# Compute engines in program order from the first network matmul on, with the steps of the transform laid out anew

## The chip, the core and the metric

The kernel runs on one core of one Trainium2 chip. The metric is the device time of one execution in microseconds, the median of several runs. Engines are TensorE (PE in the rows, its weight loads PEld), VectorE (DVE), ScalarE (ACT), GpSimd (POOL) and SyncE (SP, which here only issues DMAs).

## The reference

Three stages follow one another on 8 x 3072 tokens of 256 channels:

```
X = rfft(x, axis=1);  y = irfft(X * (filt_r + i filt_i))      # a long convolution, per batch row
h = y @ w_in                                                  # 256 -> 2048
g = h if h >= 1;  0 if h <= -1;  else (h + 1)^2 / 4
x2 = g @ w_out                                                # 2048 -> 256
e = argmax(x2 @ w_gate);  p = softmax(x2 @ w_gate)[e]          # one of 8 experts per token
out = p * (relu(x2 @ w1[e]) @ w2[e])                           # 256 -> 1024 -> 256
```

Everything is float32 at both ends.

## The kernel before

**Stages.** The transform runs one batch row at a time, as eight "transform units" u = 0 to 7. Unit 0 comes alone, ahead of the network. Then the network (the two dense layers and the routing) runs over 48 blocks of 512 tokens, and beside the blocks of unit u-1's tokens the matmuls of unit u are slipped in. After the last block come the experts, tile by tile of 256 tokens.

**Precision.** Each float32 operand is split in a high and a low part (f16 in the network and the experts, a rounded float32 in the transform), and three matmuls (high x high, high x low, low x high) stand for one. The splitting is ACT, DVE and POOL work.

**The network's loop.** A "unit" n is 256 tokens by 512 hidden columns; there are 384, of four *steps* each, 1536 steps in all. Step 4n and 4n+1 are the two halves of the first layer (`l1`, L520, 12 matmuls each, into a two-bank PSUM tile `hps`); `act1` (L535) clips on DVE (L538) and squares on ACT (L539); `act2` (L542) takes the maximum on DVE (L544), makes `gh` on ACT (L547) and `gl` on POOL (L548). Steps 4n+2 and 4n+3 are the second layer (`l2`, L551) of unit n-2, 12 matmuls each, into the two PSUM banks `yps`. After the last unit of half a block `finish` (L570) copies `yps` to `ysb`, one bank by ACT (L574), one by DVE (L575), and at the end of a block it sets events for scaling, routing (`route1`, `route2`) and scatters of the rows.

**Events.** `ev(h, f)` puts f into step h; `fire(h)` (L931) calls what lies there, between the halves of the layers. Every piece of the transform, the routing and the experts' weight preparation is such an event. In a transform unit the A pieces (`a_load`, `a_run`, six groups) transform along one axis; the B pieces (16 groups) load a table, the filter and A's result, split it (`b_split`, L397), transform it (`b_fwd`, L401), copy it turned to `xs` (ACT, L412, L413), multiply with the filter (`b_mul`: DVE L420, POOL L421), add (`b_add`: DVE L427), split the sum into `yh` and `yl` (L324 on ACT, L325 on DVE), and transform back (`b_inv`, L430). `a_inv` (L502) makes the network's input of a block. All of these, the scales and `route2` share two PSUM banks (`fps`, L165).

**What sets the order.** The program order is that of the events, but the planner that lays out each engine's queue from simulated times may move instructions past each other; only some are pinned by `keep_in_program_order`. The events' offsets are the constants at L28 to L34: B's inverse comes 5 steps after its forward transform (LG), A's load 3 steps ahead of its use (LA), `z_load` 14 and `a_inv` 11 and 6 steps ahead of the block (ZO), `route2` 4 steps after the block and one after `route1`'s second part (FO).

Of the kernel before, what the change touches and what calls it, by code (L numbers as in the profile page):

```python
# [31 lines left out]
UA = (9, 4.7)  # L32
CVA = 4
LA, LB, LC, SA, HB, SB_, LG = 3, 14, 9, 7.4, 59.8, 7.4, 5  # L34
# [95 lines left out]
def tile_kernel(ctx, tc, x, w_in, w_out, w_gate, w1, w2, cst, tab, fil, out):  # L130
# [37 lines left out]
    if True:  # L168
# [71 lines left out]
        def bmax(m, n):  # L240
            k = m.shape[0]
            p = fps()
            PE.transpose(p[0:n, 0:k], m, c[0:k, C_ID:C_ID + k])
            q = fp.tile([n, 1], F32, tag="bm", name="bm")
            V.tensor_reduce(q, p[0:n, 0:k], axis=AX.X, op=ALU.max)
            if n > 1:
                d = fp.tile([n, n], F32, tag="bd", name="bd")
                V.tensor_scalar(d, c[0:n, C_ID:C_ID + n], q, None, op0=ALU.mult)
                q = d
            p = fps()  # L250
            PE.matmul(p[:, 0:n], lhsT=c[0:n, C_ONE:C_ONE + 128], rhs=q)
            return p[:, 0:n]
# [30 lines left out]
        def scales(u):  # L283
            zm = sq[u]
            m = fp.tile([96, 1], F32, tag="zr", name="zr")
            V.tensor_reduce(m, zm, axis=AX.X, op=ALU.max)
            q = fp.tile([128, 12], F32, tag="sq", name="sq")
            qi = q.bitcast(I32)
            pow2(q[:, 0:1], bmax(m, 1), -30, 100)
# [22 lines left out]

        def warp(h):
            k, r = divmod(h - W1, 32)
            return int(32 * k + W1 + r * (32 - WL) / 32)
# [5 lines left out]
        def split(X, t, th, tl):  # L321
            h = qp.tile(list(t.shape), F32R, tag=th, name=th, bufs=bufs.get(th))
            l = qp.tile(list(t.shape), F32R, tag=tl, name=tl, bufs=bufs.get(tl))
            A.activation(h, t, AF.Copy)  # L324
            X.tensor_tensor(l, t, h.bitcast(F32), op=ALU.subtract)  # L325
            return h, l
# [19 lines left out]
        def pin(u, g, *a):  # L346
            i = SP.dma_start(*a)
            if u == 1 and g < 3:
                tc.keep_in_program_order(i)

        def fft_unit(u, ha, sa, hb, sb, lag):
# [4 lines left out]
            def a_load(g):  # L356
                xi = alt(u, g, [128, 4, D], "xi", (qp, "xi"), (fp, "zt"), (fp, "xl"), (qp, "xg"), (fp, "zt"), (fp, "xl"))
                pin(u, g, xi, x[u].rearrange("(p s) d -> p s d", s=S2)[:, 4 * g:4 * g + 4, :])
                st["x", g] = xi

            def a_run(g):
                xi = st.pop(("x", g))
                if u:
                    xg, xr = split(G, xi, "xg", "xr")
                ao = alt(u, g, [128, 4, D], "ao", (qp, "ao"), (fp, "xh"), (qp, "xr"), (fp, "xh"))
                for i in range(2):
                    p = ups(u)
                    s = slice(2 * i, 2 * i + 2)
                    if u:
                        mm(p, cah, cal, xg[:, s].rearrange("p b d -> p (b d)"), xr[:, s].rearrange("p b d -> p (b d)"))  # L370
                    else:
                        mm(p, c[:, C_A:C_A + 128], None, xi[:, s].rearrange("p b d -> p (b d)"), None)
                    A.activation(ao[:, s].rearrange("p b d -> p (b d)"), p, AF.Copy)
                SP.dma_start(s1v[:, 4 * g:4 * g + 4], ao)

            def b_load(g):
                if u:
                    tt = qp.tile([128, 2, 2, 224], F32R, tag="tt", name="tt")
                    G.dma_start(tt, tab[g, :, 1:3])
# [3 lines left out]
                tf = alt(u, g, [128, 2, 2 * D], "tf", (qp, "tf"), (fp, "xh"), (fp, "xl"))  # L383
                pin(u, g, *((tf, fil[g]) if u or g == 0 else (tf[0:64], fil[g, 0:64])))
                st["b", g] = (tt, tf)

# [10 lines left out]
            def b_split(g):  # L397
                tt, tf, t = st["b", g]
                st["b", g] += split(V, t, "ag", "al") if u else (None, None)

            def b_fwd(g):  # L401
                tt, _, t, ag, al = st["b", g]
# [13 lines left out]
            def b_mul(g):  # L416
                tf = st["b", g][1]
                pv, xs = st.pop(("p", g))
                xq = alt(u, g, [128, 2, D], "xq", (qp, "xq"), (fp, "gl"))
                V.tensor_tensor(xq, pv, tf[:, :, 0:D], op=ALU.mult)  # L420
                G.tensor_tensor(xs, xs, tf[:, :, D:], op=ALU.mult)  # L421
                st["q", g] = (xq, xs)

            def b_add(g):
                if u:
                    xq, xs = st["q", g]
                    V.tensor_tensor(xq, xq, xs, op=ALU.add)  # L427
                    st["q", g] = split(V, xq, "yh", "yl")

            def b_inv(g):  # L430
# [10 lines left out]
                z = alt(u, g, [96, 2, D], "z", (qp, "ao"), (qp, "xi"), (qp, "xg"), (qp, "xr"))  # L441
# [3 lines left out]
                V.tensor_reduce(sq[u][:, g:g + 1], z.rearrange("p q d -> p (q d)"), axis=AX.X, op=ALU.max, apply_absolute_value=True)  # L445
                SP.dma_start(s2v[8 * g:8 * g + 8].rearrange("(q p) s d -> (p s) q d", q=2), z)

            if u == 0:
# [16 lines left out]
                for g in range(NG):  # L465
# [4 lines left out]
                    at(t, (b_split, g), (b_fwd, g), (b_mul, g), (b_add, g))  # L470
# [4 lines left out]
                return  # L475
            for g in range(NA):
                h = warp(ha + sa * g)
                ev(h - LA, lambda g=g: a_load(g))
                ev(h, lambda g=g: a_run(g))
            for g in range(NG):  # L480
                h = warp(hb + g * sb)
                ev(h - LB, lambda g=g: b_load(g))
                ev(h - LB, lambda g=g: b_load2(g))
                ev(h - LC, lambda g=g: b_dup(g))
                ev(h - LC, lambda g=g: b_split(g))
                ev(h, lambda g=g: b_fwd(g))
                ev(h, lambda g=g: b_mul(g))
                ev(h, lambda g=g: b_add(g))
                ev(warp(hb + g * sb + lag), lambda g=g: b_inv(g))
# [4 lines left out]
        def z_load(k):  # L494
# [3 lines left out]
            if k < 2:  # L498
# [3 lines left out]
        def a_inv(k, kt):  # L502
# [8 lines left out]
            V.scalar_tensor_tensor(xl[:, kt, :], p, sx, xh[:, kt, :], op0=ALU.mult, op1=ALU.subtract)  # L511
# [58 lines left out]
        def finish(k, half, h):  # L570
# [7 lines left out]
            o = FO if k < NBLK - 1 else (0, 0, 0, 0, 2, 2, 2, 6, 5)  # L578
# [4 lines left out]
            ev(h + o[4], lambda: route2(k, 0))  # L583
            ev(h + o[5], lambda: route2(k, 1))
            ev(h + o[6], lambda: route1(k, 2))
            for j in range(4):
                ev(h + o[7] + o[8] * j, lambda j=j: hilo(k, j, 0))
                ev(h + o[7] + o[8] * j, lambda j=j: hilo(k, j, 1))
                ev(h + o[7] + 1 + o[8] * j, lambda j=j: scatter(k, j))
# [18 lines left out]
        def route1(k, i):  # L608
# [5 lines left out]
            if i == 0:  # L614
# [6 lines left out]
                tc.keep_in_program_order(V.memset(row[:, :, D + 2:ROW], 0.0))  # L621
# [70 lines left out]
        def wload(i):  # L692
            src, _, _, wi = wchunk(i % 64)
            t = fp.tile([128, 512], F32, tag="wst", name="wst", bufs=3)
            tc.keep_in_program_order(SP.dma_start(t if wi == 0 else t.rearrange("p (k d) -> p k d", d=D), src))
# [7 lines left out]
        def wscale():  # L703
            m = fp.tile([128, 2], F32, tag="wm", name="wm")
            V.tensor_reduce(m, wmax.rearrange("p (a b) -> p a b", a=2), axis=AX.X, op=ALU.max)
            p = fps()
# [9 lines left out]
            for a in range(2):  # L716
                V.tensor_scalar(dg[:, a, :], c[0:2, C_ID:C_ID + 2], m2[:, 2 + a:3 + a], None, op0=ALU.mult)
            p2 = fps()
# [19 lines left out]
        fft_unit(0, 0, 0, 0, 0, 0)  # L738
        z_load(0)
        scales(0)  # L740
        for f in range(UF):
            wi_split(f)
        for kt in range(2):
            a_inv(0, kt)
# [280 lines left out]
```

## Time and profile before

| | us |
|---|---|
| median of 3 runs | 3742.18 (3742.1 to 3750.3) |
| the profiled execution, its own time | 3752.54 |
| its span, first to last instruction | 3750.8 |
| PE busy | 3532.5 (94%) |
| DVE, ACT, POOL busy | 2459.9, 1807.8, 1671.1 |
| network stage (first network matmul to the last) | 140.0 to 2724.1 |

Busy is time in which at least one instruction of the engine was at work. "Idle before" in a row is the time that the engine stood still just ahead of the instructions of that row, and the arrow names what it waited for. PEclk is the share of full TensorE clock (2.4 GHz) that was granted.

### The profile page before, as it was taken

Reading aid. Unit: us, or ns where it says so; the run is one execution under the profiler, and the core shown is the slowest. Engines: PE = TensorE matmul, PEld = TensorE weight load, DVE = VectorE, ACT = ScalarE, POOL = GpSimd, SP = SyncE. Lnnn points to the kernel's source line nnn. Section 1 sums busy time; section 2 is a strip of 40 time slices with the busy share of each in tenths; the row PEclk is TensorE's granted clock in tenths of the full one; section 3 lists DMA queues with packets and bytes.
Section 4 is the critical chain, followed back from the end, with each engine's and each line's share of the span. In section 5 each row is a group of like instructions: output and inputs, shape, how many; then the busy total and the mean of one; then the engine's idle time right before and its main releaser. Section 6 shows DMA issues by size and latency. Waiting matters only on the chain. (4 is left out here: it accounts for less than half of the span.)

```text
span 3750.8 us, 75150 instructions
## 1 busy us (share of the span) xinstructions
PE 3532.5 (94%) x30690; PEld 3075.9 (82%) x30690; DVE 2459.9 (66%) x3830; ACT 1807.8 (48%) x2406; POOL 1671.1 (45%) x1154
## 2 busy tenths in 40 slices
PE   6799899999999999999999999999999999999998
PEld 4687787878778777888888788888888888888887
DVE  6678868887896887788688778867642333333222
ACT  4655555656555565665566566544422222222221
POOL 1355455555555555555555545544422222222222
PEclk7899999999999999999999999999999999999999
DMA  9345434433443443454344335301132222222221
GB/s 274 122 131 150 137 122 132 140 119 122 145 133 114 132 131 117 130 151 126 120 131 137 116 105 152 96 24 70 45 76 52 51 52 52 52 52 52 52 50 52
DMA packets 323821, 395.33 MB, mean 105 GB/s; under 512 B 163791, under 2 KB 250063, under 8 KB 322960
## 3 DMA queue, kind: packets, MB, share of 16 engines
q1 hardware_dynamic: 274848, 279.90, 26.1%
q0 software_dynamic: 48624, 110.58, 9.8%
q8 instruction: 243, 3.98, 0.5%
q14 instruction: 106, 0.87, 0.1%
HBM read 439.70 MB, written 120.49 MB: 149 GB/s over the span
## 5 line engine op out<-in xcount | busy, mean ns | idle before, releaser
L548 POOL TENSOR_TENSOR gl<-cl,gh 128x1024 f16<-128x1024 f32 x384 | 834.1, 2173 | 691.0 <-ACT gh L547 332.8
L531 PE MATMUL hps<-xh,wih 128*128 128x256 f16 x3072 | 841.6, 274 | 4.3 <-DVE cl L544 4.3
L531 PE MATMUL hps<-xl,wih 128*128 128x256 f16 x3072 | 841.2, 274 | 0.7 <-DVE xl L511 0.7
L531 PE MATMUL hps<-xh,wil 128*128 128x256 f16 x3072 | 841.0, 274 | 0.0
L561 PE MATMUL yps<-woh,gh 128*128 128x264 f16 x3072 | 730.1, 278 | 11.7 <-ACT ysb L574 6.6
L561 PE MATMUL yps<-wol,gh 128*128 128x264 f16 x3072 | 730.7, 279 | 0.0
L539 ACT ACTIVATE cl<-cl,sq 128x1024 f32<-128x1024 f32 x384 | 475.9, 1239 | 493.2 <-DVE cl L538 455.1
L561 PEld LDWEIGHTS <-gh 128*128 128x128 f16 x6144 | 592.5, 99 | 115.7 <-issue 21.9
L886 DVE SCALAR_TENSOR_TENSOR hl<-mh,hh 128x1024 f16<-128x1024 f32 x194 | 237.6, 1225 | 655.6 <-ACT hh L885 655.5
L531 PEld LDWEIGHTS <-wih 128*128 128x128 f16 x6144 | 595.9, 98 | 86.4 <-DVE cl L544 5.8
L544 DVE SCALAR_TENSOR_TENSOR cl<-hps,sq,cl 128x1024 f32<-128x1024 f32 x384 | 491.2, 1279 | 198.8 <-ACT cl L539 197.3
L538 DVE TENSOR_SCALAR cl<-hps,sq 128x1024 f32<-128x1024 f32 x384 | 513.2, 1337 | 118.6 <-PE hps L531 114.7
L547 ACT ACTIVATE gh<-cl 128x1024 f16<-128x1024 f32 x384 | 404.9, 1055 | 312.9 <-DVE cl L544 304.6
L877 PE MATMUL mh<-xt,wslot 128*128 128x256 f16 x4656 | 540.2, 273 | 0.0
L885 ACT ACTIVATE hh<-mh 128x1024 f16<-128x1024 f32 x194 | 198.4, 1023 | 655.0 <-PE mh L877 450.9
L877 PEld LDWEIGHTS <-wslot 128*128 128x128 f16 x4656 | 455.6, 98 | 52.9 <-issue 0.2
L561 PE MATMUL yps<-woh,gl 128*128 128x264 f16 x3072 | 420.8, 278 | 1.6 <-POOL gl L548 1.6
L900 PE MATMUL my<-wslot,hh 128*128 128x256 f16 x3104 | 371.4, 273 | 0.4 <-issue 0.3
L561 PEld LDWEIGHTS <-gl 128*128 128x128 f16 x3072 | 299.5, 98 | 52.5 <-POOL gl L548 2.9
L900 PEld LDWEIGHTS <-hh 128*128 128x128 f16 x3104 | 303.7, 98 | 36.0 <-issue 1.0
L531 PEld LDWEIGHTS <-wil 128*128 128x128 f16 x3072 | 301.8, 98 | 37.8 <-issue 0.9
L677 POOL DMA_INDIRECT rows<-row,posi x192 | 206.0, 1073 | 270.6 <-DMA rows<-row,posi 97.6
(202 smaller groups left out, 4361.1 us busy)
## 6 DMA issues: line engine op xcount, KB each, us to landing
tf<-in_fil_dram SPq DMA_DIRECT2D x113, 512.0 KB
tt<-in_tab_dram POOLq DMA_DIRECT2D x112, 448.0 KB
wst<-in_w_dram SPq DMA_DIRECT2D x128, 256.0 KB
xi<-in_x_dram SPq DMA_DIRECT2D x48, 512.0 KB
scr<-ao SPq DMA_DIRECT2D x48, 512.0 KB
a<-scr SPq DMA_DIRECT2D x128, 192.0 KB
scr<-z SPq DMA_DIRECT2D x128, 192.0 KB
zt<-scr SPq DMA_DIRECT2D x48, 512.0 KB
```

Of the source, the lines that this page charges most:

```text
L531: PE.matmul(p[:, i, :], lhsT=w[:, kt, f * 128:(f + 1) * 128], rhs=xx[:, kt, s], start=a == 0, stop=a == 5)
L538: V.tensor_scalar(cl, p, q[:, 5:6], q[:, 3:4], op0=ALU.max, op1=ALU.min)
L539: A.activation(cl, cl, AF.Square, bias=q[:, 11:12], scale=q[:, 4:5])
L544: V.scalar_tensor_tensor(cl, p, q[:, 7:8], cl, op0=ALU.mult, op1=ALU.max)
L547: A.activation(gh, cl, AF.Copy)
L548: G.tensor_tensor(gl, cl, gh, op=ALU.subtract)
L561: PE.matmul(yps[j][:, 0:WO], lhsT=gg[:, i, j * 128:(j + 1) * 128], rhs=w[:, f, :], start=f == 0 and first, stop=f == NF - 1 and gg is gl)
L677: G.indirect_dma_start(out=rows, out_offset=IOA(ap=posi[:, j:j + 1], axis=0), in_=row[:, j, :], in_offset=None, bounds_check=NROWS - 1, oo ...
L877: PE.matmul(p[:, i, :], lhsT=w[:, wo + kt * FE + f * 128:wo + kt * FE + f * 128 + 128], rhs=xt_[:, xo + kt, :], start=a == 0, stop=a == 5)
L885: A.activation(hh, p, AF.Relu)
L886: V.scalar_tensor_tensor(hl, p, 0.0, hh, op0=ALU.max, op1=ALU.subtract)
L900: PE.matmul(yq[t][j][:, 0:D], lhsT=hx[:, i, j * 128:(j + 1) * 128], rhs=w[:, wo + f * D:wo + (f + 1) * D], start=f == 0 and first, stop=f ...
```

## The change

The whole of what follows unit 0's transform is put under a manual schedule of PE, DVE, ACT and POOL: their queues follow the program order, and the planner lays out SP's queue alone. The pinning of single instructions goes, but for two loads.

The events are laid out anew. Each use of the two `fps` banks gets a step of its own: a heap of wished-for steps is worked off, and each use takes the first step that is later than the last one given away, at which one of two banks is free (a use holds its bank for 3 to 5 steps), and at which its inputs and buffers allow it. A's pieces come one half group per slot, with the split done 9 and 8 steps ahead (6 and 5 in unit 1). B's parts are spread over the steps after the forward transform. `act2` of a unit moves from ahead of the second layer's steps to behind them. The low part of B's input (`al`) moves from DVE to POOL. More buffers (`more`, pool `qx`) take the place of the weight staging tiles once these are done.

```diff
-W1, WL = 9, 1
-FO = (0, 2, 2, 3, 4, 5, 6, 11, 3)
-ZO = (14, 11, 5, 7, 3)
-LA, LB, LC, SA, HB, SB_, LG = 3, 14, 9, 7.4, 59.8, 7.4, 5
+AL, AX1, AX2 = 15, 9, 8
+BL, BS1, BS2, BM, BV, BZ = 14, 9, 8, 1, 9, 2
+BC = ((3, 6, 7, 9, 11, 6), (3, 7, 8, 10, 13, 8))
+A1, A2 = (4, 3.5), (-50, 5.0)
+B1, B2 = (60, 5.6), (26, 7.9)
+ZL, ZB, AI, XL = 20, 8, (17, 12), 2
+RT = (1, 2, 4, 6, 11, 4, 17, 18, 20, 24, 3)
...
+            def b_lo(g):
+                _, _, t, ag, al = st["b", g]
+                G.tensor_tensor(al, t, ag.bitcast(F32), op=ALU.subtract)
...
+            def b_slot(s, g):
+                sb.append(s)
+                ev(s - BL, lambda: b_load(g))
+                ev(s - BL, lambda: b_load2(g))
+                ev(s - BT, lambda: b_tab(g))
+                ev(s - BS1, lambda: b_hi(g))
+                ev(s - BS2, lambda: b_lo(g))
+                ev(s, lambda: b_fwd(g))
+                ev(s + BM, lambda: b_mul(g, 0))
+                ev(s + BX, lambda: b_mul(g, 1))
+                ev(s + BA, lambda: b_add(g))
+                ev(s + BH, lambda: b_yh(g))
+                ev(s + BLO, lambda: b_yl(g))
+                slot(s + BI, lambda s: i_slot(s, g))
+
+            def i_slot(s, g):
+                si.append(s)
+                ev(s, lambda: b_inv(g))
+                ev(s + BZ, lambda: b_zm(g))
+                if g == NG - 1:
+                    ev(s + BZ + 1, lambda: scales(u, s + BZ + 1))
+                    ev(s + ZB, lambda: z_load(6 * u))
+                    for kt in range(2):
+                        slot(s + BZ + 10 + 5 * kt, lambda s, kt=kt: inv_slot(s, 6 * u, kt), 5)
...
-        scales(0)
+        region = ExitStack()
+        region.enter_context(tc.manual_schedule(engines={mybir.EngineType.PE, mybir.EngineType.DVE, mybir.EngineType.Activation,
+                                                         mybir.EngineType.Pool}))
         for f in range(UF):
             wi_split(f)
+        scales(0)
...
         for f in range(NF):
-            ev(f + 1, lambda f=f: wo_split(f))
-        ev(NF + 1, wt.close)
+            ev(f - f // 8, lambda f=f: wo_split(f))
+        ev(NF - 2, qx_open)
         for k in range(1, NBLK):
             h = 2 * k * NF
...
+            slot(h + 7 + RT[4], lambda s, k=k: (ev(s, lambda: route2(k - 1, 0)), ev(s + RT[5], lambda: route2(k - 1, 1))))
...
+        while slots:
+            t, _, fn, hold, bound = heapq.heappop(slots)
+            b = bound() if bound else 0
+            if b is None or b > t + 1:
+                slot(t + 1 if b is None else b, fn, hold, bound)
+                continue
+            s = max(round(t), last + 1, min(free), b)
+            last, free = s, [s + hold, max(free)]
+            fn(s)
...
             fire(4 * n + 1)
-            if mo < 0:
-                act2(n, pc)
             for part in range(2):
                 if n >= LAG:
                     if n - LAG < NU:
...
                 if part == 0:
                     fire(4 * n + 2)
+            if mo < 0:
+                act2(n, pc)
             fire(4 * n + 3)
         order.close()
+        region.close()
```

The last two numbers but one of a BC tuple are `yl`'s step (9 or 10) and the inverse's (11 in unit 1, 13 in the others), counted from the forward transform.

## Rows read from the trace of the kernel before

**Rows 1.** The page: busy share of PE in 40 slices, tenths
```profile
PE   6799899999999999999999999999999999999998
```
**Rows 2.** Windows of the stages: window, length, busy us (instructions) per engine, PEclk, DMA
```profile
0.00:140.00 140.00, 89.35 (x335) 63.87 (x335) 102.53 (x220) 71.49 (x119) 27.88 (x24) 0.78 0.78 231
140.00:2725.00 2585.00, 2432.03 (x21098) 2106.64 (x21097) 2041.40 (x3160) 1491.91 (x1992) 1350.96 (x838) 0.99 0.39 119
2725.00:3751.00 1026.00, 1011.09 (x9261) 905.41 (x9259) 316.01 (x452) 244.41 (x295) 292.27 (x292) 1.00 0.24 54
```
**Rows 3.** Groups of PE, 140 to 2725: count | busy, mean ns | idle before, releaser
```profile
L531 PE MATMUL hps<-xh,wih 128*128 128x256 f16 x3072 | 841.6, 274 | 4.3 <-DVE cl L544 4.3
...
L561 PE MATMUL yps<-woh,gh 128*128 128x264 f16 x3072 | 730.1, 278 | 11.7 <-ACT ysb L574 6.6 <-DVE ysb L575 5.0
...
L333 PE MATMUL fps<-yh,tt 128*96 128x256 f32 x448 | 115.2, 309 | 65.4 <-ACT yh L324 65.1
L333 PE MATMUL fps<-ag,tt 96*128 96x256 f32 x448 | 107.1, 300 | 3.2 <-DVE xl L511 3.0
L509 PE MATMUL fps<-c,zt 128*128 128x128 f32 x753 | 105.6, 283 | 18.2 <-DMA zt<-scr 15.0 <-ACT ao L373 2.9
L333 PE MATMUL fps<-yl,tt 128*96 128x256 f32 x224 | 73.4, 328 | 19.8 <-DVE yl L325 19.5
...
L333 PE MATMUL fps<-xg,cah 128*128 128x512 f32 x84 | 37.7, 454 | 6.0 <-DVE xl L511 3.5 <-ACT ao L373 2.5
...
L648 PE MATMUL fps<-oh,tri 128*128 128x40 f16 x47 | 8.7, 185 | 18.6 <-DVE oh L634 14.3 <-DVE gt L635 2.2 <-DVE xq L420 1.8
```
**Rows 4.** Windows of 100 us: the first and last of 25, 200 to 2700
```profile
200.00:300.00 100.00, 92.94 (x799) 80.03 (x797) 81.12 (x129) 56.15 (x77) 52.77 (x33) 0.97 0.45 135
...
2600.00:2700.00 100.00, 94.72 (x845) 83.36 (x843) 70.14 (x124) 46.66 (x55) 47.89 (x29) 0.98 0.29 92
```
**Rows 5.** Groups of ACT, POOL and DVE, 140 to 2725: B's chain
```profile
L412 ACT ACTIVATE xs<-fps 64x512 f32<-64x512 f32 x112 | 66.5, 594 | 2.7
L413 ACT ACTIVATE xs<-fps 64x512 f32<-64x512 f32 x112 | 65.9, 588 | 1.3
...
L421 POOL TENSOR_TENSOR xs<-xs,tf 128x512 f32<-128x512 f32 x112 | 156.3, 1395 | 114.5 <-issue 57.0 <-ACT xs L413 56.7 <-POOL gl L548 0.6
...
L427 DVE TENSOR_TENSOR xq<-xq,xs 128x512 f32<-128x512 f32 x112 | 119.6, 1068 | 25.6 <-POOL xs L421 24.0
...
L324 ACT ACTIVATE yh<-xq 128x512 fp32r<-128x512 f32 x112 | 69.7, 623 | 85.6 <-DVE xq L427 83.7 <-issue 1.5
...
L325 DVE TENSOR_TENSOR yl<-xq,yh 128x512 fp32r<-128x512 f32 x112 | 109.2, 975 | 0.1
```
**Rows 6.** Groups of DVE, 140 to 2725: routing chain, first and last of five
```profile
L630 DVE TENSOR_TENSOR eq<-eq,c 128x32 f32<-128x32 f32 x47 | 25.7, 547 | 0.0
...
L634 DVE TENSOR_TENSOR oh<-c,m 128x32 f16<-128x32 f32 x47 | 8.4, 180 | 0.0
```
**Rows 7.** Groups of POOL and DVE, 140 to 2725; then L325 alone: ns min/median/max
```profile
L548 POOL TENSOR_TENSOR gl<-cl,gh 128x1024 f16<-128x1024 f32 x384 | 834.1, 2173 | 691.0 <-ACT gh L547 332.8 <-issue 248.0 <-PE hps L531 56.6
...
L575 DVE COPY ysb<-yps 128x264 f32<-128x264 f32 x96 | 40.6, 423 | 31.7 <-PE yps L561 31.7
...
L325 DVE TENSOR_TENSOR al<-a,ag 96x512 fp32r<-96x512 f32 x112 | 126.0, 1125 | 23.0 <-ACT ag L324 23.0
...
L325 DVE TENSOR_TENSOR al<-a,ag x112: 674/680/4081, 210.9 to 2394.2; 96x512 fp32r<-96x512 f32 x112
```
**Rows 8.** Timeline, 118 to 142: start, us, instruction, count, idle before
```profile
121.18 5.69 ACT L272 ACTIVATE wih<-wi,wq 128x256 f16<-128x256 f32 x14 [1.23 <-DVE wq L259]
...
124.89 4.44 DVE L273 SCALAR_TENSOR_TENSOR wil<-wi,wq,wih 128x256 f16<-128x256 f32 x11
...
132.73 2.91 DVE L279 SCALAR_TENSOR_TENSOR wol<-wo,wq,woh 128x264 f16<-128x264 f32 x7
...
132.86 0.32 PE L243 MATMUL fps<-c,zr 96*1 96x96 f32 x1 [10.53 <-DVE zr L286]
```

More of the change, by code (lines that the diff above doesn't have):

```diff
@@ L238, in cv_lg, with bmax, first, second @@
             V.tensor_reduce(wmx[:, 2, 2 * j:2 * j + 2], w, axis=AX.X, op=ALU.max, apply_absolute_value=True)
-        def bmax(m, n):
+        def bmax(m, n, steps=None):
             k = m.shape[0]
[L242 to L252, printed above, removed]
+            t = {}
+            def first():
+                t["p"] = fps()
+                PE.transpose(t["p"][0:n, 0:k], m, c[0:k, C_ID:C_ID + k])
+            def second():
+                q = fp.tile([n, 1], F32, tag="bm", name="bm")
+                V.tensor_reduce(q, t["p"][0:n, 0:k], axis=AX.X, op=ALU.max)
+                if n > 1:
+                    d = fp.tile([n, n], F32, tag="bd", name="bd")
+                    V.tensor_scalar(d, c[0:n, C_ID:C_ID + n], q, None, op0=ALU.mult)
+                    q = d
+                t["q"] = q
+            def third():
+                p = fps()
+                PE.matmul(p[:, 0:n], lhsT=c[0:n, C_ONE:C_ONE + 128], rhs=t["q"])
+                return p[:, 0:n]
+            if steps is None:
+                first()
+                second()
+                return third()
+            return first, second, third
         def pow2(o, i, lo, hi):
@@ L347, in pin, with fft_unit @@
             i = SP.dma_start(*a)
-            if u == 1 and g < 3:
+            if u == 1 and g == 0 and a[0].name.startswith("xi"):
                 tc.keep_in_program_order(i)
-        def fft_unit(u, ha, sa, hb, sb, lag):
+        def fft_unit(u):
             s1v, s2v = scr1[u % 2], scr2[u % 2]
@@ L356, in a_load @@
             def a_load(g):
+                if u:
+                    first = u == 1 and g < 4
+                    xi = more(0 if first else g, 1, 0 if first else 1, [128, 4, D], F32, "xi")
+                    pin(u, g, xi, x[u].rearrange("(p s) d -> p s d", s=S2)[:, 4 * g:4 * g + 4, :])
+                    st["x", g] = xi
+                    return
                 xi = alt(u, g, [128, 4, D], "xi", (qp, "xi"), (fp, "zt"), (fp, "xl"), (qp, "xg"), (fp, "zt"), (fp, "xl"))
@@ L478, in fft_unit @@
-                ev(h - LA, lambda g=g: a_load(g))
-                ev(h, lambda g=g: a_run(g))
+                for i in range(2):
+                    slot(h + a0 + asp * (2 * g + i), lambda s, g=g, i=i: a_slot(s, g, i), 3, lambda i=2 * g + i: a_bound(i))
             for g in range(NG):
[L481 to L489, printed above, removed]
+                slot(h + b0 + bsp * g, lambda s, g=g: b_slot(s, g), 4, lambda g=g: b_bound(g))
+        slots = []
+        def slot(t, fn, hold=3, bound=None):
+            heapq.heappush(slots, (t, nslot[0], fn, hold, bound))
+            nslot[0] += 1
+        nslot = [0]
+        xgp = []
         zt = {}
```

207 lines of the change are left out of this document (144 added, 63 removed).

## The prediction

> **What bounds the kernel now.** I read the page's slices first, then the busy time by stage, then PE's groups by what they waited for, then the windows' clock. The slices show PE at seven tenths or more from the second one on, and at nine or more almost throughout [rows 1], so PE sets the time and the question is where it still stands still. By stage [rows 2]: the 140 us before the network have PE busy for 89.35; the expert stage from 2725 us on has it busy for 1011.1 of 1026, the rest being the end of the program; the network stage has it busy for 2432.0 of 2585.0. So 153.0 us of standing still lie in the network stage. The other engines are not full there: DVE 2041.4 of 2585 (79%), ACT 1491.9 (58%), POOL 1351.0 (52%). PE's waits are therefore waits for order and latency, not for a full engine.
>
> PE's groups of that stage [rows 3] name them. Nearly all stand ahead of matmuls of the transform and the routing, not of the network: `yh` 65.4 and `yl` 19.8 (B's inverse transform, waiting for ACT's and DVE's splits), `route2` 18.6, `a_inv` 18.2 (mostly the load of `zt`), A 6.0, B's forward 3.2. The network's own waits are 11.7 (the copies of `yps`) and 4.3. That is 147.2 of the 153.0; the other 5.8 lie in groups too small to show.
>
> The clock adds a second loss. In the 25 windows of 100 us from 200 to 2700 PEclk reads 1.00 nine times, 0.98 thirteen times and 0.97 three times; the first and the last stand in [rows 4]. The shortfalls add up to 0.35 of a window, 35 us of full speed lost to short spells at 1.2 GHz; where PE is never idle, in the expert stage, it is 1.00 [rows 2]. What can be won at most is 153 + 35 = 188 us.
>
> **The change part by part.** The sum is made against the profiled execution, 3752.5 us (span 3750.8), which is 10.3 us over the median of 3742.2; at the end I take the same difference from the median. A step is now 2585 / 1536 = 1.68 us on average, and without the waits (2585 - 188) / 1536 = 1.56 us.
>
> *B's inverse (85.2 us of waits).* From forward to inverse there are two `xs` copies on ACT (0.594 + 0.588), the product on POOL (1.395), the sum on DVE (1.068), `yh` on ACT (0.623), `yl` on DVE (0.975) [rows 5]: 5.24 us if none waits in a queue. The five steps of before give 5 x 1.68 = 8.4 us, 3.2 us to spare, less than one `gl` (2.173) and one DVE operation held up. The new layout gives 11 steps in unit 1 and 13 later, 17.2 and 20.3 us, 12 to 15 us to spare. The worst single delay that I see on DVE is an `al` of 4.081 us against a median of 0.680 [rows 7], and three of these fit. I leave a tenth, 8 us (bounds 0 and 85).
>
> *`route2` (18.6).* Its one-hot comes from five DVE operations of 0.547 to 0.180 us [rows 6], under 2.8 us in all. Before there is one step, 1.7 us, between the two; now there are at least five, 7.8 us. I leave 1 us (0 to 19).
>
> *`a_inv` (18.2).* The waits for `zt` come at the first block of a transform unit, where the load can only start once the last inverse has been written out. The distance from load to use goes from three steps (5.0 us) to four (6.2 us), and a late load still stops PE. I leave 5 us (0 to 18).
>
> *A, B's forward and the small rest (6.0 + 3.2 + 5.8 = 15.0).* These are mostly waits for a bank of `fps` that DVE or ACT has not read out. With a slot per use and 3 to 5 steps (4.7 to 7.8 us) of hold, against readers of about 1 us, I leave 3 us (0 to 15).
>
> *The network's own waits (11.7 + 4.3 = 16.0), and new ones.* `yps` must be copied between the last step of a half block and the next step of the second layer, two steps or 3.1 us on, and the DVE copy takes 0.423 us [rows 7]: 2.7 us of slack, the shortest in the new order. In a strict queue whatever DVE was given in the two steps before stands ahead of this copy, and behind it stand the maximum of `act2` and then the next clip, for which ACT, POOL and in the end PE wait. `act2` itself moves by two steps, but PE needs `gh` only eight steps, 12.5 us, after the clip, so I cost that at nothing; its cover is the slack of those steps. Nothing in the trace of before shows what strict order costs here. Below, it is a gain of 16 us (all these waits go); above, each of the 96 copies would stop PE for 2 us, 192 us. I take 30, near the 16.0 measured, since DVE has 20% to spare.
>
> *`al` from DVE to POOL.* DVE loses 126.0 us; POOL gets 112 operations of, by the nearest row, 1.395 us, 156 us, and goes from 1351 to about 1507 of some 2450 us, 62%. Neither is near full, so I cost it at nothing by itself; what it does to the other DVE operations is the second rival's.
>
> A DVE operation with both inputs in SBUF is held up while POOL works: `al` has a minimum of 0.674, a median of 0.680 and a maximum of 4.081 us [rows 7], while `gl` alone keeps POOL for 2.173. The Trainium skill, "SBUF — State Buffer", section "Who interferes with whom", has the rule: VectorE with two SBUF inputs and GpSimd reading SBUF share a port, and the second to start "fully blocks" until the first is done. By that rule moving work to POOL takes DVE time away from the sums and `yl` that stay, and the time would be that of the second rival.
>
> *Start of the network.* Before, the weight splits run ahead of the network, while PE waits 10.53 us for the scales; ACT's 14 splits (5.69 us) and DVE's 11 (4.44 us) stand in front of the last pieces of unit 0 [rows 8]. In program order most splits come after the scales, in steps -2 to 14. That brings the scales forward by up to 5 us, and puts 12 x 0.40 + 16 x 0.42 = 11.5 us of DVE work (per operation 4.44 / 11 and 2.91 / 7) into the first steps, beside four units' clips and maxima. I take a loss of 2 us (from a gain of 5 to a loss of 12).
>
> *Expert stage.* PE is busy throughout and each engine's order there is already that of the data: 0 (plus or minus 3).
>
> *Sum.* Waits left: 8 + 1 + 5 + 3 + 30 = 47, so 153 - 47 = 106 us go. The spells of half clock I scale with the waits: 35 x 106 / 153 = 24 us back. With the 2 us of the start: 106 + 24 - 2 = 128 us. 3752.5 - 128 = 3624.5 for a profiled execution, 3742.2 - 128 = **3614 us** for the median.
>
> **The rivals.**
>
> *Nearly all of it goes.* Every piece has 5 us or more to spare, and no strict queue backs up. Then 188 us go: 3742 - 188 = 3554 us. For it speaks that all waits but 16 us are in pieces whose distance grows; against it the short slack of the `yps` copies. Chance 0.18.
>
> *DVE falls behind through POOL's load.* POOL goes from 52% to 62%, and the 224 sums and `yl` that stay on DVE run into it more often, with `gl` and `al` back to back up to 2.2 + 1.4 us. In a strict queue the clip and maximum behind them are late too. If one in five of the 224 comes through to PE at 1.5 us, that is 67 us: 3614 + 67 = 3681 us. For it speaks the mean of 1.125 for `al` against a median of 0.680, against it that DVE loses 126 us of work. Chance 0.13.
>
> *Slower: strict order stops PE at each `yps` copy.* Place: the end of each half block, 96 times. With a lag of 4.7 us in DVE's queue PE would stand for 2 us each time: 192 us in place of the 30, so 3614 + 162 = 3776, and with the clock's 24 us not given back 3800 us. It decides from (30 + 128) / 96 = 1.6 us per copy on, a lag of 4.3 us at every half block. For it speaks that a single held operation can take 4.1 us; against it that this is the maximum of 112 and DVE is at 79%. Chance 0.11.
>
> *The change doesn't do what it says.* SP's queue is still the planner's, without most pins; if loads of A's result, the tables or `zt` come later by as much as the compute order wins, PE waits for DMAs instead: about 3740 us. PE waited for `zt` for 15.0 us before [rows 3], so that is not excluded, but the loads of A and `zt` are called earlier now. Chance 0.04.
>
> **How the numbers follow.** The forecast has 0.54, with its own range of 3575 to 3660. The range that should hold 8 in 10 takes in the full gain and the second rival and leaves out the last two cases and the tails: 3548 to 3700. Faster by over 0.3%, about what a measurement of this kernel can tell from no change (11 us, under 3731): 0.54 + 0.18 + 0.13 = 0.85; within it 0.04; slower 0.11.
>
> **What would show it.** In the changed profile the waits ahead of `yh` and `yl` together should be under 20 us, those of `route2` under 4, PE in the network stage busy for 97% or more, and PEclk at 1.00 in most windows of 100 us. The waits ahead of the second layer's first matmul (on `ysb`) tell the slower rival, long sums and `yl` on DVE with waits for the clips the second one, waits of `a_inv` or B's forward on DMAs the last. The prediction is wrong if PE's standing still in the network stage is over 100 us, or if it has gone and the expert stage has grown.

## The result: 1.2% slower, and where the 41 us came in

The changed kernel takes 3787.6 us (3783.9 to 3794.0, four runs) against 3742.1 us: a ratio of 1.0122, 95% interval 1.0098 to 1.0145. The forecast was 3614 with a range up to 3700; it is wrong in sign and size.

PE's slices (page of the kernel after, tenths of busy time), against [rows 1]:

```profile
PE   6698999899999999999999999999989999999997
```

The second slice has gone from 7 to 6 (the end of the start and the network's first block), the single 8 among the blocks (the fifth slice) has become two (the fourth and the eighth), and the 30th is new at 8 (2749 to 2844 us, where the network hands over to the experts). By stage (windows of the kernel after: window, length, busy us per engine PE, PEld, DVE, ACT, POOL, then PEclk, DMA share, GB/s), against [rows 2]:

```profile
0.00:135.00 135.00, 87.13 (x332) 61.75 (x333) 87.36 (x179) 59.06 (x89) 23.13 (x21) 0.79 0.82 246
135.00:2742.00 2607.00, 2438.36 (x21090) 2114.45 (x21090) 2074.81 (x3079) 1499.84 (x2064) 1505.00 (x993) 0.98 0.39 117
2742.00:3792.00 1050.00, 1015.90 (x9273) 907.83 (x9270) 310.44 (x462) 244.62 (x296) 294.71 (x294) 0.99 0.23 53
```

The network stage stands still for 2607.0 - 2438.4 = 168.6 us where 153.0 stood before, and the clock has not risen, it has fallen a little (0.981 to 0.974 over the whole span). The expert stage, which had no waits to speak of, is 24 us longer, and PE's standing still there, the end of the program included, goes from 14.9 to 34.1.

Cut at the first network matmul of each of the 48 blocks (my division of the two profiled executions, us; their spans differ by 41.4, the medians by 45.5):

| part | before | after | difference |
|---|---|---|---|
| start, to block 0 | 140.0 | 135.4 | -4.5 |
| block 0 | 50.2 | 77.4 | +27.2 |
| blocks 1 to 41, beside the transforms | 2248.9 | 2234.9 | -14.0 |
| blocks 42 to 45, no transform left | 182.0 | 177.9 | -4.1 |
| block 46 to the first expert matmul | 92.1 | 105.9 | +13.8 |
| expert matmuls | 1023.2 | 1043.6 | +20.4 |
| end | 14.2 | 17.1 | +2.9 |
| span | 3750.8 | 3792.2 | +41.4 |

So there are two questions. Why do the 41 blocks for which the order was laid out gain only 14 us? And why do block 0 and the switch to the experts lose 27 and 34?

**The 41 blocks.** PE's groups of 135 to 2742 us in the kernel after (line, engine, operation, tiles, shapes, count | busy us, mean ns | idle before, what ended it), against [rows 3]:

```profile
L667 PE MATMUL hps<-xh,wih 128*128 128x256 f16 x3072 | 848.1, 276 | 12.9 <-DVE cl L680 12.6 <-ACT xh L640 0.3
...
L697 PE MATMUL yps<-woh,gh 128*128 128x264 f16 x3072 | 729.3, 279 | 1.3 <-ACT ysb L710 0.7 <-DVE ysb L711 0.5
L697 PE MATMUL yps<-woh,gl 128*128 128x264 f16 x3071 | 411.3, 277 | 7.5 <-POOL gl L684 7.5
...
L356 PE MATMUL fps<-ag,tt 96*128 96x256 f32 x448 | 111.9, 311 | 34.6 <-ACT z L508 26.7 <-DMA tt<-in_tab_dram 3.2 <-ACT ag L447 2.7
L356 PE MATMUL fps<-yh,tt 128*96 128x256 f32 x448 | 110.4, 304 | 4.8 <-DVE xl L641 3.3 <-ACT yh L486 1.5
L639 PE MATMUL fps<-c,zt 128*128 128x128 f32 x756 | 105.3, 284 | 23.2 <-ACT ao L415 17.9 <-DVE xq L474 4.3 <-ACT z L508 0.5
L356 PE MATMUL fps<-yl,tt 128*96 128x256 f32 x224 | 67.8, 303 | 63.9 <-DVE yl L492 63.9
L356 PE MATMUL fps<-xg,cah 128*128 128x512 f32 x84 | 40.7, 484 | 15.2 <-ACT ao L415 6.3 <-ACT xg L404 5.1 <-DVE eq L769 2.7
```

The 65.4 us ahead of `yh` have become 63.9 ahead of `yl`: the wait has changed its name, from ACT's half of the split to DVE's. The waits on `ACT z` (26.7) are new, those on `ACT ao` have grown from 5.4 to 24.2. They are waits for a bank of `fps` not yet read out. The waits for the copies of `yps` are almost gone (11.7 to 1.3), so the place that the slower rival named is not the one.

DVE's groups of the same stretch show why `yl` is late:

```profile
L492 DVE TENSOR_TENSOR yl<-xq,yh 128x512 fp32r<-128x512 f32 x112 | 123.2, 1100 | 0.0
L481 DVE TENSOR_TENSOR xq<-xq,xs 128x512 f32<-128x512 f32 x112 | 100.9, 901 | 16.7 <-POOL xs L477 16.4
L474 DVE TENSOR_TENSOR xq<-fps,tf 128x512 f32<-128x512 f32 x112 | 77.0, 688 | 109.4 <-ACT xs L466 109.2
```

`yl` itself never waits (0.0). DVE waits 109.2 us at the product `xq`, which the new order puts one step behind the forward transform, for ACT's second copy of the same bank; before it was 8.4 (kernel before, 140 to 2725 us):

```profile
L420 DVE TENSOR_TENSOR xq<-fps,tf 128x512 f32<-128x512 f32 x112 | 76.1, 679 | 8.5 <-ACT xs L413 8.4
```

While DVE waits, everything behind it in program order waits too. One such stall, in the timeline of the kernel after (start us, length us, instruction, idle before and its releaser), in the order DVE, ACT, PE:

```profile
982.34 0.69 DVE L474 TENSOR_TENSOR xq<-fps,tf 128x512 f32<-128x512 f32 x1 [2.47 <-ACT xs L466]
982.95 1.33 DVE L674 TENSOR_SCALAR cl<-hps,sq 128x1024 f32<-128x1024 f32 x1
984.20 0.68 DVE L492 TENSOR_TENSOR yl<-xq,yh 128x512 fp32r<-128x512 f32 x1
...
979.51 1.06 ACT L683 ACTIVATE gh<-cl 128x1024 f16<-128x1024 f32 x1 [1.40 <-DVE cl L680]
980.48 0.61 ACT L486 ACTIVATE yh<-xq 128x512 fp32r<-128x512 f32 x1
981.12 0.59 ACT L465 ACTIVATE xs<-fps 64x512 f32<-64x512 f32 x1
981.72 0.59 ACT L466 ACTIVATE xs<-fps 64x512 f32<-64x512 f32 x1
...
984.94 0.36 PE L356 MATMUL fps<-yl,tt 128*96 128x256 f32 x1 [1.85 <-DVE yl L492]
```

Read it from the bottom. PE stands 1.85 us for `yl`. The inputs of `yl` were there at 981.09, when ACT ended `yh`, but DVE had the product of the *next* slot at its head and waited 2.47 us for that slot's two copies. ACT made these behind `gh` and `yh`, and had itself waited 1.40 us at `gh` for DVE's maximum. Two queues in strict order pass one delay back and forth. Over all 112 pieces `yl` starts 2.0 us after the end of its `yh` on average, before it was 1.05, and in e3, below, it is 1.02 (my pairing of the traces). The Trainium skill, "PSUM — Partial Sum Buffer", section "Engine vs sequencer instructions", says that the queues of VectorE and ScalarE are strictly first in, first out. The trace agrees: `yl` starts at 984.20, 3.1 us after its data were there. What the change took away is the planner's choice of what stands ahead of what in these queues; below, "strict order" means that the queue follows the program.

**Block 0** is read from experiment e5 and **the switch** from e6. The largest wait at the switch (timeline of the kernel after) is

```profile
2763.98 1.22 PE L1065 MATMUL my<-wslot,hh 128*128 128x256 f16 x5 [8.41 <-ACT o L1077]
```

PE waits for ACT's copy of the first expert outputs. That needs the gates from DVE, and DVE is in the second routing list, about 10 us of small operations issued in one place (the first and the last of it, then the gates):

```profile
2752.62 0.16 DVE L999 CAST basei<-base 128x8 int32<-128x8 f32 x1
...
2762.88 0.15 DVE L1010 TENSOR_SCALAR tot<-pf 128x1 int32<-128x1 f32 x1
...
2763.14 0.22 DVE L1072 TENSOR_SCALAR gs<-me,winv 128x2 f32<-128x2 f32 x1
```

It is not the only new wait. Between the first and the last expert matmul PE stands still for 0.4 us before and for 17.2 us after, and half of that is for the loads of expert weights (`wslot`), in four places up to 3757 us (pages of the kernel before and of the kernel after):

```profile
L877 PE MATMUL mh<-xt,wslot 128*128 128x256 f16 x4656 | 540.2, 273 | 0.0
```

```profile
L1042 PE MATMUL mh<-xt,wslot 128*128 128x256 f16 x4656 | 541.6, 273 | 8.3 <-DMA wslot<-wsc,widx 8.3
L1065 PE MATMUL my<-wslot,hh 128*128 128x256 f16 x3104 | 372.1, 273 | 8.9 <-ACT o L1077 8.9
```

### The profile page after: what moved, and what is told of

Same layout as the page of the kernel before. It is cut to its first block, busy times and chain, and to the rows that moved or that the text cites. A ratio compares the mean times of both kernels' runs of the same rounds, so it can differ in the third digit from the quotient of the medians.

```text
span 3792.2 us, 75013 instructions
## 1 busy us (share of the span) xinstructions
PE 3541.4 (93%) x30690; PEld 3084.0 (81%) x30690; DVE 2472.6 (65%) x3718; ACT 1803.5 (48%) x2448; POOL 1822.8 (48%) x1308
## 5 line engine op out<-in xcount | busy, mean ns | idle before, releaser
L667 PE MATMUL hps<-xh,wih 128*128 128x256 f16 x3072 | 848.1, 276 | 12.9 <-DVE cl L680 12.6
L680 DVE SCALAR_TENSOR_TENSOR cl<-hps,sq,cl 128x1024 f32<-128x1024 f32 x384 | 490.6, 1278 | 108.4 <-ACT cl L675 104.2
L1080 POOL DMA_INDIRECT out_dram<-o,me x194 | 190.8, 984 | 706.7 <-ACT o L1077 465.4
L697 PE MATMUL yps<-woh,gl 128*128 128x264 f16 x3072 | 411.4, 277 | 7.5 <-POOL gl L684 7.5
```

The source lines that it names most:

```text
L667: PE.matmul(p[:, i, :], lhsT=w[:, kt, f * 128:(f + 1) * 128], rhs=xx[:, kt, s], start=a == 0, stop=a == 5)
L680: V.scalar_tensor_tensor(cl, p, q[:, 7:8], cl, op0=ALU.mult, op1=ALU.max)
L697: PE.matmul(yps[j][:, 0:WO], lhsT=gg[:, i, j * 128:(j + 1) * 128], rhs=w[:, f, :], start=f == 0 and first, stop=f == NF - 1 and gg is gl)
L1080: G.indirect_dma_start(out=out, out_offset=IOA(ap=me.bitcast(I32)[:, tk, 1:2], axis=0), in_=o, in_offset=None, bounds_check=NTOK - 1, oob_ ...
```

## The experiments

Each kernel is the changed one with the edit shown, unless the text says otherwise; ratios are to the kernel before.

**e1 and e2: layout and strict order apart.** e1 keeps the new layout and leaves out the region of manual order, so the planner orders the engines. e2 puts the region around the old layout and drops the pin of one small operation on DVE.

```diff
 e1
-        region = ExitStack()
-        region.enter_context(tc.manual_schedule(engines=...))
 e2 (kernel before)
+        region = ExitStack()
+        region.enter_context(tc.manual_schedule(engines=...))
         for f in range(UF):
             wi_split(f)
```

> The new layout of the steps, with the queues of the compute engines given back to the planner (no manual schedule before the experts). Theory 1 (strict order: whatever waits at the head of an in-order queue holds up all behind it, and a piece's slack counts from its own place in the queue): the planner can move ready work past a waiting piece, so the waits of PE in the network stage fall well under the 145 us of the changed kernel, and the losses of the first block (27 us) and of the tile list (8 us) go: 3700 us, 3680 to 3730. Theory 2 (the low part moved to GpSimd holds up VectorE at the shared port): the port is as loaded as in the changed kernel, so 3770 us or more.

> The kernel before with its old layout, its compute queues in program order. Theory 1: the old layout has forward transform, product and sum in one step, so VectorE waits at each of the 112 groups for the whole chain (some 4 us), and the clips behind it as well: over 3900 us. Theory 2: GpSimd has no more work than before, so only the start and the list are lost: about 3790 us.

e1 took 3875.2 us (1.0365, 1.0341 to 1.0388), e2 5154.0 us (1.3781, 1.3741 to 1.3820). e2 came out over 3900, as expected, and far over. e1 missed: it is slower than the strict order, and its time lies in the range that its expectation gave to the port. The switch (92.6) and the expert matmuls (1022.9) are what they were before the change, so the loss there comes with strict order and not with the layout. Of the start that holds in part: start and block 0 together take 146.5 + 57.4 = 203.9 us, against 190.2 before and 212.8 after. Blocks 1 to 41 take 2353.3. PE's groups of e1, 200 to 2700 us:

```profile
L667 PE MATMUL hps<-xh,wih 128*128 128x256 f16 x2834 | 787.0, 278 | 80.8 <-DVE cl L680 80.2
...
L697 PE MATMUL yps<-woh,gh 128*128 128x264 f16 x2839 | 682.0, 281 | 93.9 <-ACT ysb L710 56.6 <-DVE ysb L711 36.6 <-ACT gh L683 0.8
```

The network's own work, the maximum and the copies of `yps`, now comes late on DVE and ACT. So neither half of the change is good without the other (the new layout takes in `al` on POOL, more buffers and fewer pins): old layout with planner 3742, old layout strict 5154, new layout with planner 3875, both new 3788. Why the planner puts other work ahead of the copies was not tried. The port is not excluded as a part of it: in e1 the sums on DVE take 1899 ns each, in the kernel after 901.

**e3: the product two steps later.** It is aimed at DVE's wait at the head of its queue.

```diff
-BL, BS1, BS2, BM, BV, BZ = 14, 9, 8, 1, 9, 2
+BL, BS1, BS2, BM, BV, BZ = 14, 9, 8, 3, 9, 2
```

> The changed kernel with the first product (VectorE, reads the bank after ScalarE's two copies) three steps behind the forward transform instead of one. Theory 1: VectorE's 113 us of waiting for the copies at the head of its queue fall under 30, PE's waits for the low part yl fall from 64 to under 25 us, and the time goes from 3788 to about 3745 us (3730 to 3765). Theory 2: the port decides, 3780 to 3795 us.

3760.7 us (1.0053, 1.0035 to 1.0072), 27 us under the changed kernel. DVE's groups of e3, 135 to 2742 us, then PE's group of `yl`, 200 to 2700 us:

```profile
L492 DVE TENSOR_TENSOR yl<-xq,yh 128x512 fp32r<-128x512 f32 x112 | 161.1, 1439 | 2.8 <-ACT yh L486 2.8
...
L474 DVE TENSOR_TENSOR xq<-fps,tf 128x512 f32<-128x512 f32 x112 | 76.2, 680 | 1.0 <-ACT xs L466 1.0
```

```profile
L356 PE MATMUL fps<-yl,tt 128*96 128x256 f32 x224 | 67.0, 299 | 43.7 <-DVE yl L492 43.6
```

The head wait is gone (109.2 to 1.0), but only 20 us of PE's wait for `yl` go with it, less than expected. Two or three steps from `yl` to the inverse are still too few, the more so as `yl` itself now takes 1439 ns in place of 1100, which no run takes apart. And the product now holds its bank longer: 23.5 us of waits on it came in ahead of `yh`.

**e7: the inverse two steps later.** The other end of the same chain.

```diff
-BC = ((3, 6, 7, 9, 11, 6), (3, 7, 8, 10, 13, 8))
+BC = ((3, 6, 7, 9, 13, 6), (3, 7, 8, 10, 15, 8))
```

> The changed kernel with B's inverse transform two steps later and nothing else moved: yl then has four or five steps from its own place in the queue to its use instead of two or three. If slack counts from a piece's own place, PE's waits for yl fall from 64 to under 20 us and the time to about 3745 us (3730 to 3760). If it counts from the forward transform on, as the prediction had it, two more of 13 steps change nothing: 3780 to 3795.

3790.3 us (1.0134, 1.0109 to 1.0159): no gain. The time lies in the range that the expectation gave to slack counted from the forward transform; the waits do not fit that. PE's groups of e7, 200 to 2640 us:

```profile
L697 PE MATMUL yps<-woh,gh 128*128 128x264 f16 x2908 | 693.5, 280 | 21.9 <-DVE ysb L711 19.2 <-ACT ysb L710 2.7
...
L356 PE MATMUL fps<-ag,tt 96*128 96x256 f32 x448 | 112.1, 312 | 73.4 <-ACT z L508 37.9 <-DMA tt<-in_tab_dram 18.2 <-issue 17.4
L356 PE MATMUL fps<-yh,tt 128*96 128x256 f32 x448 | 108.4, 304 | 20.1 <-ACT ao L415 20.0
...
L356 PE MATMUL fps<-yl,tt 128*96 128x256 f32 x224 | 64.1, 286 | 12.4 <-DVE yl L492 12.4
```

The wait for `yl` falls from 63.9 to 12.4, under the 20 expected, so its slack does count from its own place; but the same time comes back ahead of the forward transforms, `yh` and the copies of `yps`. DVE still waits 86.5 us (whole trace) for `xs` at its head. Slack at the end of the chain moves the wait; it does not make DVE or ACT earlier.

**e4: `al` back on DVE**, against the rival that POOL's load is what holds DVE up.

```diff
-                G.tensor_tensor(al, t, ag.bitcast(F32), op=ALU.subtract)
+                V.tensor_tensor(al, t, ag.bitcast(F32), op=ALU.subtract)
```

> The changed kernel with the low part of B's input (al) back on VectorE. Theory 2: VectorE's other two-input operations are held up less (the rows' low part from 846 towards 600 ns, yl from 1100 towards 950), PE's waits fall and the time with them: 3755 us or less. Theory 1: 112 operations of about 1 us more in VectorE's strict queue, so no gain: 3785 to 3830 us.

3828.9 us (1.0233, 1.0207 to 1.0259), 41 us *over* the changed kernel. The row product of the gather (L812) and `al`, whole trace, e4 first, then the kernel after:

```profile
L812 DVE SCALAR_TENSOR_TENSOR row<-ysb,sm,row 128x256 f16<-128x256 f32 x192 | 134.2, 700 | 3.2 <-ACT row L810 3.2
...
L452 DVE TENSOR_TENSOR al<-a,ag 96x512 fp32r<-96x512 f32 x112 | 101.7, 908 | 28.1 <-ACT ag L447 28.1
```

```profile
L812 DVE SCALAR_TENSOR_TENSOR row<-ysb,sm,row 128x256 f16<-128x256 f32 x192 | 160.2, 835 | 3.1 <-ACT row L810 3.0
...
L452 POOL TENSOR_TENSOR al<-a,ag 96x512 fp32r<-96x512 f32 x112 | 151.5, 1353 | 25.5 <-ACT ag L447 20.8 <-PE fps L356 3.5
```

With `al` on DVE the row product drops from 835 to 700 ns, so having `al` on POOL does slow it. But the relief is smaller than the work: over the network stage DVE is busy for 2112.8 us in e4 and for 2074.8 in the kernel after, 38 us more for an `al` of 101.7, and `al` waits 28.1 us for ACT at the head of the queue. As the cause of the loss the move of `al` falls; what the rest of POOL's work costs DVE was not tried.

**e5: all weight splits ahead of the region**, so none stands in the queue between the first clips and maxima.

```diff
+        for f in range(NF):
+            wi_split(f)
+        for f in range(NF):
+            wo_split(f)
         region = ExitStack()
...
-        for f in range(UF, NF):
-            ev((f - UF) * 3 // 4 - 2, lambda f=f: wi_split(f))
-        for f in range(NF):
-            ev(f - f // 8, lambda f=f: wo_split(f))
```

> The changed kernel with all weight splits ahead of the manual schedule, where the planner lays them into the gaps of unit 0's end. If the 27 us of the first block are the splits in VectorE's and ScalarE's strict queue beside the first units, the first block takes about 50 us as before and the time goes to about 3765 us (3760 to 3772). If it is the transform's pieces in the first block (A of unit 1), it stays at 3780 or more.

3764.4 us (1.0079, 1.0053 to 1.0104), 23 us under the changed kernel. The first windows, e5 and then the kernel after:

```profile
141.00:193.00 52.00, 47.75 (x380) 38.99 (x380) 23.04 (x22) 26.37 (x36) 22.86 (x15) 0.96 0.32 107
```

```profile
135.00:213.00 78.00, 54.51 (x382) 41.74 (x382) 45.18 (x65) 39.47 (x64) 23.27 (x15) 0.84 0.23 75
```

The same 380 matmuls take 52 us in place of 78, though they begin 5.8 us later; beside the waits PE's granted clock was 0.84 there (0.96 in e5).

**e6: the routing lists in pieces**, two small operations of each per step over 12 and 14 steps, and the loads of the first three tiles' expert weights (`m_w`) ten steps later. The two were not tried apart.

```diff
-        ev(h, list1)
+        pieces(h - 2, 12, 2, list1)
...
-            ev(h + 2 + t, lambda t=t: m_w(t))
+            ev(h + 12 + t, lambda t=t: m_w(t))
...
-        ev(h2 + 6, list2)
+        pieces(h2 + 6, 14, 2, list2)
```

> The changed kernel with the two tile lists (some 40 small VectorE operations each, issued in one step) spread two and two over 14 steps. If the lists as a block in the strict queue cost the 12.9 us of waits at the change to the experts and the spells of half clock behind them, 3770 us (3762 to 3776); if those are the scatters and weight loads on GpSimd's queue, 3783 or more.

3760.6 us (1.0063, 1.0036 to 1.0090), 27 us under the changed kernel, more than expected. The switch is back at 91.1 us (105.9 after, 92.1 before) and the experts at 1036.3 (1043.6 after, 1023.2 before). PE's groups of e6 with waits, 2640 to 2790 us, then the expert matmuls on its page:

```profile
L1086 PE MATMUL my<-wslot,hh 128*128 128x256 f16 x192 | 23.9, 279 | 3.1 <-ACT o L1098 3.1
L697 PE MATMUL yps<-woh,gl 128*128 128x264 f16 x112 | 14.9, 277 | 2.8 <-POOL gl L684 2.8
```

```profile
L1063 PE MATMUL mh<-xt,wslot 128*128 128x256 f16 x4656 | 541.8, 273 | 6.1 <-DMA wslot<-wsc,widx 6.0
L1086 PE MATMUL my<-wslot,hh 128*128 128x256 f16 x3104 | 371.6, 273 | 3.6 <-ACT o L1098 3.6
```

**e9: the maximum's step ahead of the second layer's again** (`act2` back to its old place).

```diff
             fire(4 * n + 1)
+            if mo < 0:
+                act2(n, pc)
             for part in range(2):
...
-            if mo < 0:
-                act2(n, pc)
             fire(4 * n + 3)
```

> The changed kernel with act2 (the maximum on VectorE, gh, gl) called ahead of the second layer's steps again, as before the change. If what stands at the head of a strict queue decides, VectorE now waits for ScalarE's square (1.24 us) behind each of the 384 clips: its waits of the maximum for the square grow from 104 to 300 us or more and the time to 3830 us or more. If act2's later place is what starves gh and gl, 3770 us or less.

3958.1 us (1.0583, 1.0557 to 1.0609), 170 us over the changed kernel. DVE's waits at the maximum for ACT's square go from 104.2 us to 275.1, a little less than expected (pages of the kernel after and of e9):

```profile
L680 DVE SCALAR_TENSOR_TENSOR cl<-hps,sq,cl 128x1024 f32<-128x1024 f32 x384 | 490.6, 1278 | 108.4 <-ACT cl L675 104.2
```

```profile
L680 DVE SCALAR_TENSOR_TENSOR cl<-hps,sq,cl 128x1024 f32<-128x1024 f32 x384 | 491.9, 1281 | 279.1 <-ACT cl L675 275.1
```

One instruction ahead of the second layer's matmuls instead of behind them, 384 times, is the dearest of the single edits to the new kernel.

**e8, e10 to e12: the mended kernel.** e8 joins e3, e5, e6 and e7 and holds a B slot for 5 steps in place of 4; e10 also calls the tables three steps earlier for the later units; e11 is e8 with the hold back at 4; e12 is e8 with `al` on DVE as in e4.

```diff
 e10 (over e8; b_tab's distance BT is the last of the tuple)
-BC = ((3, 6, 7, 9, 13, 6), (3, 7, 8, 10, 15, 8))
+BC = ((3, 6, 7, 9, 13, 6), (3, 7, 8, 10, 15, 11))
```

> All four at once: splits ahead of the manual schedule, lists spread, the first product three steps behind the forward transform (and that bank held a step longer), the inverse two steps later. If the losses are separate, 3788 - 22 - 17 - 27 - 40 = 3682 us (3670 to 3705), well under the kernel before. If they stand in for each other (another wait takes the place of each), 3720 us or more.

> The kernel with all four edits, and from unit 2 on the loads of B's tables called 11 steps ahead of the forward transform instead of 8. PE's 27.6 us of waits ahead of that transform for the table or its issue should fall under 8, and the time from 3662 to 3640 us (3632 to 3650). If the wait only moves (to the bank that ScalarE's copy of z frees), 3655 to 3668.

> The kernel with all four edits, but the bank of the forward transform counted as free after 4 steps, as in the changed kernel, though the product reads it 3 steps on. If the late product blocks the next use of the bank, as the single edit with the product moved showed (23.5 + 12.2 us of PE's waits on it), 3675 to 3700 us; if the inverse's two steps alone made the difference, 3655 to 3668.

> The kernel with all four edits, but with al on VectorE. If VectorE's queue is short of time as such (its work and its hold-ups at the port), the 112 operations more cost what they cost in the changed kernel, some 40 us: 3690 to 3710. If only the waits at the head of the queue, now gone, made it short, 3660 to 3672. If the port were what the change lost by, 3650 or less.

| | us | ratio (95%) | block 0 | 1 to 41 | switch | experts |
|---|---|---|---|---|---|---|
| after | 3787.6 | 1.0122 (1.0098 to 1.0145) | 77.4 | 2234.9 | 105.9 | 1043.6 |
| e8 | 3662.2 | 0.9794 (0.9771 to 0.9816) | 51.5 | 2152.9 | 93.0 | 1036.8 |
| e11 | 3669.8 | 0.9806 (0.9783 to 0.9828) | 53.3 | 2157.0 | 93.3 | 1033.0 |
| e12 | 3713.4 | 0.9932 (0.9907 to 0.9956) | 51.6 | 2201.6 | 92.8 | 1033.5 |
| e10 | 3626.4 | 0.9693 (0.9667 to 0.9719) | 51.4 | 2114.1 | 92.7 | 1033.6 |

e8 gains 125 us, where the four edits by themselves add up to 27 + 23 + 27 - 3 = 74. Blocks 1 to 41 lose 82 us in e8; alone e3 takes 32 from them and e7 adds 6. e8's time lies under both ranges of its expectation. e11 lies between its two ranges and cannot be told from e8, so the hold is not what made the difference; e8's other edits touch block 0 and the switch (alone they took 7 and 5 us from these blocks). By elimination that leaves the two later steps together: e3 makes DVE early, e7 gives `yl` room, and each alone leaves the other as the limit. A run with these two alone was not made. PE's groups of `yl` and of B's forward in e8, 187 to 2640 us, of B's forward in e10, and in e10 the window of the network stage:

```profile
L356 PE MATMUL fps<-yl,tt 128*96 128x256 f32 x224 | 63.5, 283 | 0.0
...
L356 PE MATMUL fps<-ag,tt 96*128 96x256 f32 x448 | 108.6, 305 | 42.5 <-DMA tt<-in_tab_dram 14.0 <-issue 13.6 <-ACT z L508 11.1
```

```profile
L356 PE MATMUL fps<-ag,tt 96*128 96x256 f32 x448 | 108.1, 304 | 25.8 <-issue 10.3 <-ACT z L508 7.4 <-DMA tt<-in_tab_dram 6.1
```

```profile
136.60:2583.50 2446.90, 2387.77 (x21090) 2090.31 (x21089) 2041.71 (x3035) 1481.90 (x2036) 1498.43 (x993) 1.00 0.41 125
```

Nothing is left ahead of `yl`. In e10 PE stands still for 2446.9 - 2387.8 = 59.1 us of the network stage, at a clock of 1.00. The wait on tables was the next in line, but it fell only from 27.6 to 16.4 us, not under 8, while the time fell by 36, more than expected; in blocks 1 to 41 PE stands still for 50.3 us in place of 75.6, and the copies of `yps` are a part of that (12.4 to 4.8). e12 shows that `al` belongs on POOL also in the mended kernel (+51 us, a little over the range expected of a DVE short of time). e10 beats both kernels, by 3.1% and 4.3%.

## Why the prediction was wrong, step by step

*What bounds the kernel* was right: PE's waits in the network stage, and 94 us of them (153.0 to 59.1) and most of the clock could be had, as e10 shows. That e10 ends 12 us from the forecast time is luck: it has edits of the start, the lists and the tables that the sum did not count on.

*B's inverse (forecast 8 us, measured 4.8 + 63.9 = 68.7)* is the step that failed. I counted the slack from the forward transform, 11 or 13 steps, as if each piece of the chain started when its data were there. In a strict queue a piece starts at its own place: `yl` stands at step 9 or 10, so it has two or three steps, 3 to 5 us, and DVE came later than that, because its head waited 109.2 us for ACT. Neither the length of the chain nor the worst held operation, with which I bounded it, was the quantity that decided: two steps more at the use took the wait for `yl` to 12.4 (e7), the head wait gone took it to 43.7 (e3), and e8, which holds both, has it at 0.0.

*`route2` (1):* 0.0, right. *`a_inv` (5):* 23.2. The wait for `zt` did go, and 17.9 us on `ACT ao` came in its place: ACT is late too. *A, B's forward and the rest (3):* 15.2 + 4.8 + 34.6 = 54.6, mostly banks that ACT's `z` and `ao` free late (14.5 of it, 11.4 and 3.1 of A, in block 0). This is the second term that failed by far, nearly as much as the first. The hold of 4.7 us and more was set against readers of 1 us, again without the queue ahead of the reader. e7 and e8 show `ACT z` going up with the inverse alone and down to 11.1 us once both steps are moved.

*The network's own waits (30):* 12.9 + 1.3 + 7.5 = 21.7, near by luck. The copies of `yps`, which I took for the shortest slack and for which the 30 stood, cost 1.2 us; the rest is maxima and `gl`, 8.4 us in block 0 and 11.5 from block 42 on.

*`al` (0):* DVE's busy time in blocks 1 to 41 went from 1822.1 to 1829.6 us, though 126 us had left it. Longer `row` products (83.5 to 138.7 us there) and `yl` (109.2 to 123.2) took back 69 of these 133, other operations the rest. Even so the move pays: with `al` on DVE the same order takes 41 to 51 us more (e4, e12).

*The start (-2):* 27.2 - 4.5 = 22.7 us lost, nearly twice the bound of 12. The bound held only DVE's work, not that the splits stand between clip and maximum with PE waiting behind, nor the clock. *The experts (0, plus or minus 3):* 34 us lost at the switch and after. I said that the order there was that of the data, and looked at no burst of small operations in one place; e6 brings 22 of the 34 back, and 5 more before the switch. Some 13 us of the experts' 20 remain in e6 and 10 in e10. In e6 PE's waits are 9.7 of the 13, 6.0 of them for loads of expert weights, and in e10 8.9, 4.9 of them for these loads; e1, with the planner, has 0.2 in all. Why the loads come late in strict order was not tried.

*The clock (24 back):* it followed the waits, as I had it, and so was lost: over the same 25 windows from 200 to 2700 us the shortfalls add up to 0.44 of a window (0.35 before).

*The rivals.* The sign was that of the slower rival, strict order, but not its place. The second rival named DVE behind its work, which is so, but by the move of `al`, which e4 excludes as the cause; of its signs `yl` is longer (975 to 1100 ns) and the sums are shorter (1068 to 901). The rival of late DMAs is not it in the changed kernel (3.2 us on tables, under 1 on `zt`); the tables come up only once `yl` has room (e7, e8).

## What to carry to other kernels

Where an engine runs in program order, give each instruction the place at which its inputs are already there, and count its slack from that place to its use, not from the start of its chain. A wait on an engine that is not the bottleneck is paid by everyone behind it in its queue, and by the bottleneck if it needs one of these: look for the idle time at the head of such queues, and give room to the user as well. Here the first alone gained 27 us and the second alone nothing; the kernel with both, and with the two ends mended, gained 125. Spread bursts of small operations over the steps. And lay out the order together with handing over its control: either half alone was slower than the whole change.

## What the hardware showed that was not expected

Work moved from DVE to POOL comes back in part. In the same order, e4 against after, DVE's busy time in the network stage differs by 38 us for an `al` of 101.7; in the mended kernel, e12 against e8, by 17 us (2109.8 against 2092.6) for an `al` of 142.6 (e12, whole trace):

```profile
L452 DVE TENSOR_TENSOR al<-a,ag 96x512 fp32r<-96x512 f32 x112 | 142.6, 1273 | 42.1 <-ACT ag L447 41.9
```

The Trainium skill, "SBUF — State Buffer", section "Who interferes with whom", has a rule for this, a read path that DVE's two-input operations share with POOL; the row product's 835 and 700 ns agree with it. From before to after DVE stayed as busy in blocks 1 to 41 (1829.6 against 1822.1 us), but that is not the port alone: e4, with `al` still on DVE, has 1867.5 there, so the rest of the change costs DVE 45 us by itself.

So DVE was relieved of a good third and of an eighth of the moved work, and yet the time differs by 41 us (e4) and 51 us (e12). Busy time alone is not what the move was worth. On DVE `al` also waits at the head of the queue for ACT, 28.1 us in e4 and 42.1 in e12; whether that makes up the difference no run shows.
